# Routing steps in another order and one ring of twenty tiles for the attention output, in a fused attention and mixture-of-experts kernel

## The chip, the cores and the metric

The kernel runs on one core of a Trainium2 chip. The metric is the device time of one execution in microseconds; what is given is the median of the timed runs. One further execution was taken with the hardware profiler; all views below are of it.

## The reference

Chunked attention over 8 batches, 8 heads, 576 tokens and a head size of 64, then a mixture of experts (MoE) with noisy top-2 routing over the 8 x 576 = 4608 tokens of width 512:

```python
scores = scale * np.matmul(q_c, k_c.transpose(0, 1, 2, 4, 3))     # chunks of 64 tokens
scores = scores - np.max(scores, axis=-1, keepdims=True)
attn = np.exp(scores)
attn = attn / (np.sum(attn, axis=-1, keepdims=True) + 1e-09)
out = np.matmul(attn, v_c)
...
logits = x @ w_gate
noise_scale = np.log1p(np.exp(x @ w_noise))
noisy_logits = logits + noise_scale * noise
top2 = np.argpartition(-noisy_logits, 2, axis=1)[:, :2]
top2_l = np.take_along_axis(noisy_logits, top2, axis=1)
top2_l = top2_l - top2_l.max(-1, keepdims=True)
top2_w = np.exp(top2_l)
top2_w /= top2_w.sum(-1, keepdims=True) + 1e-09
for e in range(E):
    for k in range(2):
        mask = top2[:, k] == e
        h = np.maximum(x[mask] @ w1[e], 0.0)
        out[mask] += top2_w[mask, k, None] * (h @ w2[e])
```

There are 8 experts with a hidden size of 1024. All is float32.

## The kernel before, in words

The 4608 tokens are 36 tiles of 128 (a tile is one token per partition). The kernel has two stages, which overlap a little.

**Attention and routing.** `attend(it)` (line 726 on) is one iteration of a software pipeline, written out by hand; the engines run their instructions in the order in which this function issues them. In iteration `it` TensorE (PE) computes the scores of tile it+1 (L443), the product of the probabilities with V for tile it-2 (`pv`, L472), the transpose of the probabilities of tile it-1 (L460) and of the finished rows of tile it-3 (L488). Once in four iterations (`it % 4 == 3`) it multiplies four tiles with the gate weights (`gate_mm`, L500), and in the next iteration it turns those logits (`gate_turn`, L510). VectorE (DVE) takes the row maximum (`soft_max`, L448) and the difference (`soft_sub`, L453), up to three steps of routing, then the reciprocal (L480) and the normalisation of tile it-2 (`norm_c`, L483), which writes the tile's finished rows `xs`, then up to three more steps of routing. ScalarE (ACT) does the exponentials and the copies out of PSUM. The PSUM bank pair that `pv` writes is the one that `norm_c` of the tile before reads.

**Routing.** `route(g)` (L520) is a generator: each `yield` names the engine of the next step ("dve", "act", "pe") or asks to wait for the next iteration ("wait"). `step_route` lets it go on at fixed places of `attend`. It works on a group of four tiles (the last group has eight): softplus of the noise scale (L541 to L545), noise and logits (L547, L549), for each tile the eight largest values and their places (MAX at L555, MAX_INDEX at L559, recorded by the profile as MAX8 and as MATCH_VALUE_LOAD with FIND_INDEX8), the one-hot rows `oh` of the two chosen experts (L563 to L567), a running count by matmul (L577, L579), the two weights (L587, L590, L607), and last the row numbers `lii` (L610) to which the tokens go. When a group is through, its tiles are put on the list `pending`.

**Scattering.** `scatter` (L633) takes one entry of that list and issues on GpSimd (POOL) two short memsets (L640), a copy of one value that acts as a gate on an early result of the same iteration (L642), and an indirect DMA (L644) that writes the 128 rows of one tile, with code and weights behind each row, to the DRAM buffer `slots`; each tile is written twice, once for each of its two experts. `attend` calls it twice per iteration. Parts of `slots` are filled with zeros ahead of that, on the queue of SyncE (SP).

**The row buffers.** `rows` is a pool of five buffers, each of four tiles of 520 columns. `x_next(u)` (L435), called in the second half of every fourth iteration, takes the next buffer and sets one unused column to zero (L438). This memset is the first write to the buffer, so it stands on DVE behind the eight indirect DMAs that read the buffer's former content; the `norm_c` behind it need not wait for them any more.

**The MoE.** Tokens are gathered from `slots` by expert in blocks; x and both weight matrices are split into a high and a low part (`w_split` for the weights, L88 on ACT and L89 on DVE or POOL), and PE makes three matmuls of each product (L239). PE transposes gathered rows in `x_tile` (L222). Blocks 0 and 1 belong to the first expert and are gathered early, after groups 3 and 6 have been scattered (`load_early`, L666, gather at L171 on SP). Scatters that are left over after attention are issued between the matmuls of the first blocks. The output is accumulated by indirect DMA (L206).

Of the kernel before, what the change touches and what calls it, by code (L numbers as in the profile page):

```python
# [8 lines left out]
FT = mybir.dt.float32  # L9
# [4 lines left out]
AF = mybir.ActivationFunctionType  # L14
# [5 lines left out]
P = 128  # L20
NTOK = 4608
NT = NTOK // P
# [12 lines left out]
CODE, WA, WB, USED = DM, DM + 1, DM + 2, DM + 3  # L35
# [14 lines left out]
def kernel(ctx, tc, qT, kT, vh, wgn, noise, w1, w2, out, caps=CAPS):  # L50
    nc = tc.nc
# [15 lines left out]
    def w_load(e, which, c):  # L67
        st = stage.tile([P, 1024], FT, name="st")
        staged[e, which, c] = st
        if which == 1:  # L70
            if e == 0:
                nc.sync.dma_start(st, w1[0, c * P:(c + 1) * P, :])
            else:
                for j in range(4):
                    nc.sync.dma_start(st[32 * j:32 * j + 32], w1v[ds(place[e], 1), c, j].rearrange("o r f -> (o r) f"))
        else:
            nc.sync.dma_start(st.rearrange("p (f n) -> p f n", f=2),
                              w2[ds(place[e], 1) if e else slice(0, 1), 2 * c * P:(2 * c + 2) * P, :]
                              .rearrange("o (f p) n -> p (o f) n", f=2))
# [256 lines left out]
    pk = ExitStack()  # L336
    pv_pools = ExitStack()
    last_rows = ExitStack()
    rows = last_rows.enter_context(tc.tile_pool(name="rows", bufs=5, side="right"))
    gx = pa.enter_context(tc.tile_pool(name="gx", bufs=2, side="right"))  # L340
    work = pv_pools.enter_context(tc.tile_pool(name="work", bufs=3, side="right"))
    vs = pv_pools.enter_context(tc.tile_pool(name="vs", bufs=1, side="right"))
# [7 lines left out]
    def load_qk(j):  # L350
        if j < NT // 2:
            QB[j] = loads.tile([P, 2, 4, P], FT, name="qb", bufs=RING)
            for h in range(2):
                nc.sync.dma_start(QB[j][h::2], qT[HALF[h], 2 * j:2 * j + 2])
                nc.sync.dma_start(KB[j % RING][h::2, h], kT[HALF[h], 2 * j:2 * j + 2])

    def load_v(j):
        if j < NT // 2:
            for h in range(2):
                nc.sync.dma_start(VB[j % RING][h::2, h], vh[HALF[h], 2 * j:2 * j + 2])  # L360
# [66 lines left out]
    PR, PT, XS, XT, RC = {}, {}, {}, {}, {}  # L427
    by_head = lambda a: a.rearrange("p (g k h) -> p g h k", g=4, h=2)
    sco = [PS[:, b, :].rearrange("p (g h k) -> p g h k", g=4, h=2) for b in range(2)]

    def x_at(t):
        u, r = divmod(t, 4)
        return XS[u][:, r]

    def x_next(u):  # L435
        if 4 * u < NT:
            XS[u] = rows.tile([P, 4, 520], FT, name="xs")
            nc.vector.memset(XS[u][:, 0, USED:USED + 1], 0.0)  # L438

    def scores(t):  # L440
        for hp in range(4):
# [78 lines left out]
    def route(g):  # L520

        V = nc.vector
# [7 lines left out]
        y, u, sp = n3("gy"), n3("gu"), n3("gsp")  # L530
# [19 lines left out]
        m = gate.tile(n8, FT, name="gm")  # L550
# [15 lines left out]
        V.memset(ohb[:, G], 0.0)  # L566
        V.tensor_add(ohb[:, 0:G], oh[:, 0], oh[:, 1])  # L567
        ex, sm = nm("gex"), nm("gsm")
        yield "dve"
        V.tensor_sub(ex, m[:, :, 1], m[:, :, 0])  # L570
        if g == LAST:
            yield "wait"
            yield "wait"
# [3 lines left out]
        nc.tensor.matmul(rk, before, ohb, start=True, stop=False)  # L577
        for k in range(1, G + 1):
            nc.tensor.matmul(rk[:, k:G + 1], ones, ohb[:, 0:G + 1 - k], start=False, stop=(k == G))  # L579
        yield "act"  # L580
        nc.scalar.activation(ex, ex, AF.Exp)
        for x, s in parts:
            yield "dve"
            V.scalar_tensor_tensor(x.bitcast(I32)[:, :, CODE], mi[:, s, 0], 8192.0, tok[:, ts][:, s], op0=OP.mult, op1=OP.add)
        yield "wait"
        yield "dve"
        V.tensor_scalar(sm, ex, 1.0, 1e-9, op0=OP.add, op1=OP.add)  # L587
# [6 lines left out]
        yield "dve"  # L594
        r8 = n3("gr8")
        V.scalar_tensor_tensor(r8, rk[:, 0:G], 8.0, be(run8), op0=OP.mult, op1=OP.add)
        yield "dve"
        V.scalar_tensor_tensor(run8, rk[:, G], 8.0, run8, op0=OP.mult, op1=OP.add)
        yield "dve"
        ohr = gate.tile([P, 2, G, NE], FT, name="gohr")  # L600
# [65 lines left out]
    def load_early():  # L666
        for i, js, m in early:
            gather(i)
            early_loads.append(nc.sync.dma_start(
                meta0[i], by_slot[js * P:(js + m) * P, 0, CODE:USED].rearrange("(j p) c -> p j c", p=P)))  # L670
        early.clear()
# [54 lines left out]
    def attend(it):  # L726
        STEPS = 6
        if it % 2:
            load_qk((it - 1) // 2 + 3)
        if it % 2 == 0 and it >= 4:  # L730
            load_v((it - 4) // 2 + 3)
            if it == 32:
                load_early()
        if it in (9, 11):
            for r in range(CLEAN + 64 * (it // 2 - 4), CLEAN + 64 * (it // 2 - 3), 16):
                nc.sync.dma_start(slots[r * NE:(r + 16) * NE, 0:USED], zero)
        if it == 11:
            nc.sync.dma_start(slots[(CLEAN + P) * NE:NLIST * P * NE, CODE:USED].rearrange("(p r) c -> p r c", p=P),
                              zero[:, 0:3 * (NLIST * P - CLEAN - P) // 16].rearrange("p (r c) -> p r c", c=3))
        if it in range(4, 8):  # L740
            w_load(0, 1, it - 4)
        if it in (29, 31, 33, 35):
            w_load(0, 2, (it - 29) // 2)
        next_turn()
        if it == 0:
            scores(0)
        if it <= 1:
            p_trans(0) if it else scores(1)
        if it == 2:
            pv(0)  # L750
        if 0 < it < NT - 1:
            scores(it + 1)
        if 0 < it - 2 < NT:
            pv(it - 2)
        gated = it - 4 >= 0 and (it - 4) % 4 == 3
        if gated:
            gate_mm((it - 4) // 4)
        if 0 < it - 1 < NT:
            p_trans(it - 1)
        if 0 <= it - 3 < NT:  # L760
            x_trans(it - 3)
        if it - 5 >= 0 and (it - 5) % 4 == 3:
            gate_turn((it - 5) // 4)
            if grp_of[it - 5] != grp_of.get(it - 4):
                r = route(grp_of[it - 5])
                routing.append([r, next(r)])
        step_route("pe")
        if 0 <= it - 2 < NT:
            norm_a(it - 2)
        if 0 <= it - 1 < NT:  # L770
            p_copy(it - 1)
        if it < NT:
            mx = soft_max(it)
            soft_sub(it, mx)
            scatter(1, mx[0:1, 0, 0:1])
            soft_exp(it)
        if 0 <= it - 3 < NT:
            x_copy(it - 3)
        if gated:
            gate_copy((it - 4) // 4)  # L780
        step_route("dve", STEPS // 2)
        if 0 <= it - 2 < NT:
            norm_b(it - 2)
            scatter(1, RC[it - 2][0:1, 0, 0])
            norm_c(it - 2)
        if it - 5 >= 0 and (it - 5) % 4 == 3:
            gate_sum((it - 5) // 4)
        step_route("act")
        step_route("dve", STEPS // 2)
        if it >= 1 and (it - 1) % 4 == 0:  # L790
            x_next((it - 1) // 4)
        if it in range(33, 38):
            zero_out(3)
        if it == NT + 2:
            scatter(2, XT[(it - 3) // 4][0:1, 0, (it - 3) % 4, 0:1])
        elif it == NT + 3:
            scatter(2, LS[(it - 4) // 4][0:1, 0, 0:1])
        if it in range(7, 15):
            w_split(0, 1, *wq.pop(0), eng=nc.gpsimd)

    for it in range(NT):
# [242 lines left out]
```

## Time and profile before

| what | us |
|---|---|
| median of three timed runs (lowest, highest) | 968.83 (968.52, 969.94) |
| the profiled execution | 974.74 |
| span of its trace | 972.9 |
| busy in the span: PE / DVE / ACT / POOL | 951.2 / 457.5 / 287.3 / 236.3 |

The span runs from the first to the last record of the trace; the profiled execution's own time has some 2 us around it. PE is TensorE's matmuls, PEld its weight loads, which overlap them; DVE is VectorE, ACT ScalarE, POOL GpSimd, and SP SyncE, which only issues DMAs. In a timeline row stand the start, the duration of the merged instructions, the engine, the line of the kernel, the operation, the tile written and the tiles read, the shape, the count, and in brackets the idle time of the engine before it with what ended it. The granted clock of PE is given as a share of full speed.

### The profile page before, as it was taken

The numbers are of one execution on the slowest core, as the hardware profiler recorded it, in microseconds if no ns is written. First come the engines' busy times: TensorE is split into PE (matmuls) and PEld (weight loads), VectorE is DVE, ScalarE is ACT, GpSimd is POOL, SyncE is SP. The second block draws the span as 40 slices with busy tenths as digits, with TensorE's granted clock in tenths as the row PEclk, the third lists the DMA queues.
The fourth block names the chain that finished last, engine by engine and source line by source line (L and its number), as shares of the span: only waits on it lengthen the run. The fifth ranks groups of instructions, "written<-read, shape, count | busy, mean of one in ns | idle before, by whom it ended". The sixth has DMA issues, their size and how long they took to land. (4 is left out here: it accounts for less than half of the span.)

```text
span 972.9 us, 16180 instructions
## 1 busy us (share of the span) xinstructions
PE 951.2 (98%) x5776; PEld 846.5 (87%) x5776; DVE 457.5 (47%) x1026; ACT 287.3 (30%) x623; POOL 236.3 (24%) x426
## 2 busy tenths in 40 slices
PE   7999899999999999999999999999999999999996
PEld 6788678888897999899898989889998999899886
DVE  6798767226253542463255425443444343434311
ACT  3767553114141321241132214121312231223100
POOL 3267768430202011101111111211011011111113
PEclk9999999999999999999999999999999999999999
DMA  8999996987604632265316521652174217312213
GB/s 301 379 354 376 342 355 222 367 136 153 166 14 98 188 60 32 44 172 116 44 34 155 141 44 33 145 140 44 25 165 126 54 23 162 109 14 31 33 22 45
DMA packets 97300, 132.94 MB, mean 137 GB/s; under 512 B 23456, under 2 KB 56864, under 8 KB 97216
## 3 DMA queue, kind: packets, MB, share of 16 engines
q1 hardware_dynamic: 80160, 92.50, 31.0%
q0 software_dynamic: 16576, 38.33, 19.9%
q10 hardware_dynamic: 480, 1.05, 0.4%
q8 instruction: 46, 0.75, 0.3%
q14 instruction: 38, 0.31, 0.1%
HBM read 81.69 MB, written 50.13 MB: 135 GB/s over the span
## 5 line engine op out<-in xcount | busy, mean ns | idle before, releaser
L206 POOL DMA_INDIRECT out<-o,lid x75 | 116.7, 1557 | 647.2 <-DVE o L274 625.9
L239 PE MATMUL PS<-xh,w1h 128*128 128x384 f32 (+2 forms) x768 | 261.7, 341 | 1.9 <-issue 1.9
L239 PE MATMUL PS<-xl,w1h 128*128 128x384 f32 (+2 forms) x768 | 260.9, 340 | 0.2 <-issue 0.2
L239 PE MATMUL PS<-xh,w1l 128*128 128x384 f32 (+2 forms) x768 | 260.7, 339 | 0.0
L258 ACT ACTIVATE hh<-PS 128x384 fp32r<-128x384 f32 (+2 forms) x192 | 95.2, 496 | 463.0 <-PE PS L239 418.0
L239 PE MATMUL PS<-w2h,hh 128*128 128x512 f32 (+1 forms) x592 | 229.3, 387 | 0.0
L239 PE MATMUL PS<-w2h,hl 128*128 128x512 f32 (+1 forms) x592 | 229.1, 387 | 0.0
L239 PE MATMUL PS<-w2l,hh 128*128 128x512 f32 (+1 forms) x592 | 229.0, 387 | 0.0
L261 DVE SCALAR_TENSOR_TENSOR hl<-PS,hh 128x384 fp32r<-128x384 f32 (+2 forms) x192 | 108.6, 566 | 175.1 <-ACT hh L258 135.6
L274 DVE TENSOR_SCALAR o<-PS,lwt 128x512 f32<-128x512 f32 (+2 forms) x73 | 54.7, 749 | 224.8 <-PE PS L239 217.5
L239 PEld LDWEIGHTS PS<-xh,w1h 128*128 128x128 f32 x768 | 144.6, 188 | 8.2 <-issue 6.5
L239 PEld LDWEIGHTS PS<-xl,w1h 128*128 128x128 f32 x768 | 144.6, 188 | 2.1 <-issue 0.5
L239 PEld LDWEIGHTS PS<-xh,w1l 128*128 128x128 f32 x768 | 144.7, 188 | 1.0
L239 PEld LDWEIGHTS PS<-w2h,hl 128*128 128x128 f32 x592 | 110.8, 187 | 23.1
L239 PEld LDWEIGHTS PS<-w2l,hh 128*128 128x128 f32 x592 | 110.8, 187 | 22.2
L239 PEld LDWEIGHTS PS<-w2h,hh 128*128 128x128 f32 x592 | 110.8, 187 | 22.2
L644 POOL DMA_INDIRECT slots<-xs,lii x72 | 71.2, 989 | 26.0 <-issue 23.9
L229 ACT ACTIVATE xh<-y 128x512 fp32r<-128x512 f32 x67 | 41.2, 614 | 92.4 <-DVE y L226 90.4
L230 DVE TENSOR_TENSOR xl<-y,xh 128x512 fp32r<-128x512 f32 x67 | 44.9, 671 | 48.0 <-ACT xh L229 45.9
L443 PE MATMUL PS<-kb,qb 128*64 128x128 f32 x576 | 42.0, 291 | 9.1 <-DMA kb<-in_kT 7.1
L203 POOL MEMSET spacer<- 1x1 f32 x78 | 47.7, 612 | 0.0
L226 DVE STREAM_TRANSPOSE y<-xg 128x512 f32<-128x512 f32 x67 | 45.6, 680 | 0.0
(131 smaller groups left out, 692.8 us busy)
## 6 DMA issues: line engine op xcount, KB each, us to landing
st<-in_w SPq DMA_DIRECT2D x36, 512.0 KB
xg<-slots SPq DMA_DIRECT2D x252, 64.0 KB
st<-in_w SPq DMA_DIRECT2D x112, 128.0 KB
out<-zero SPq DMA_DIRECT2D x37, 256.0 KB
vb<-in_vh SPq DMA_DIRECT2D x36, 260.0 KB
qb<-in_qT SPq DMA_DIRECT2D x34, 256.0 KB
kb<-in_kT SPq DMA_DIRECT2D x32, 256.0 KB
xg<-slots SPq DMA_DIRECT2D x9, 256.0 KB
```

The source lines that it names most:

```text
L203: nc.gpsimd.memset(spacer, 0.0)
L206: s = nc.gpsimd.indirect_dma_start(out=to, out_offset=bass.IndirectOffsetOnAxis(ap=at[0:r], axis=0), in_=o, in_offset=None, compute_op=OP.add)
L226: nc.vector.transpose(y[:, 0:4 * r], x[:, 0:4 * r])
L229: nc.scalar.activation(oh, src, AF.Copy)
L230: nc.vector.tensor_sub(ol, src, oh.bitcast(FT))
L239: nc.tensor.matmul(p, a, b, start=first and n == 0, stop=last and n == 2)
L258: nc.scalar.activation(hh[:, 0:n], p, AF.Relu)
L261: nc.vector.scalar_tensor_tensor(hl[:, 0:n], p, 0.0, hh[:, 0:n].bitcast(FT), op0=OP.max, op1=OP.subtract)
L274: nc.vector.tensor_scalar(o[0:r], p[0:r], w, None, op0=OP.mult)
L443: nc.tensor.matmul(PS[q, t % 2, hp * P:(hp + 1) * P], QB[t // 2][:, t % 2, hp, q], KB[t // 2 % RING][:, :, t % 2, hp, q], start=True, stop ...
L644: s = nc.gpsimd.indirect_dma_start(out=slots, out_offset=bass.IndirectOffsetOnAxis(ap=lii[:, k, t0 + r:t0 + r + 1], axis=0), in_=XS[(t0 + ...
```

## The change

It has three parts, and the result is computed from the same numbers by the same operations.

1. **One ring.** The five buffers become one tile `xa` of twenty tiles of 520 columns; tile t lies at t modulo 20. `x_next` and its memset are gone. Each `norm_c` of a tile from 20 on writes its own place and itself waits for the two indirect DMAs that read the tile twenty before it.
2. **Routing steps.** The subtraction `ex` comes behind the counting matmuls instead of ahead of them, and the one ahead has no step of its own; the code (L584) is written ahead of the exponential's step; `r8` and the new count `run8` share one step. With that, routing of a group takes fewer steps: of the group whose routing begins in iteration 20 `lii` comes in the second half of iteration 24, where it came in the first half of iteration 27.
3. **First weights.** `w_split` of the first expert's first matrix is issued in iterations 6 to 13 instead of 7 to 14.

```diff
-    rows = last_rows.enter_context(tc.tile_pool(name="rows", bufs=5, side="right"))
+    rows = last_rows.enter_context(tc.tile_pool(name="rows", bufs=1, side="right"))
...
+    xa = rows.tile([P, 20, 520], FT, name="xs")
+    for u in range(NT // 4):
+        XS[u] = xa[:, 4 * (u % 5):4 * (u % 5) + 4]
+
     def x_at(t):
-        u, r = divmod(t, 4)
-        return XS[u][:, r]
-
-    def x_next(u):
-        if 4 * u < NT:
-            XS[u] = rows.tile([P, 4, 520], FT, name="xs")
-            nc.vector.memset(XS[u][:, 0, USED:USED + 1], 0.0)
+        return xa[:, t % 20]
...
         ex, sm = nm("gex"), nm("gsm")
-        yield "dve"
-        V.tensor_sub(ex, m[:, :, 1], m[:, :, 0])
         if g == LAST:
...
-        yield "act"
-        nc.scalar.activation(ex, ex, AF.Exp)
+        yield "dve"
+        V.tensor_sub(ex, m[:, :, 1], m[:, :, 0])
         for x, s in parts:
             yield "dve"
             V.scalar_tensor_tensor(x.bitcast(I32)[:, :, CODE], mi[:, s, 0], 8192.0, tok[:, ts][:, s], op0=OP.mult, op1=OP.add)
+        yield "act"
+        nc.scalar.activation(ex, ex, AF.Exp)
...
         V.scalar_tensor_tensor(r8, rk[:, 0:G], 8.0, be(run8), op0=OP.mult, op1=OP.add)
-        yield "dve"
         V.scalar_tensor_tensor(run8, rk[:, G], 8.0, run8, op0=OP.mult, op1=OP.add)
...
-        if it >= 1 and (it - 1) % 4 == 0:
-            x_next((it - 1) // 4)
...
-        if it in range(7, 15):
+        if it in range(6, 14):
             w_split(0, 1, *wq.pop(0), eng=nc.gpsimd)
```

How the order of instructions moves is shown at three places. The first is DVE from the end of iteration 21 to the normalisation of iteration 22 (tile 20), where the first used buffer is opened again. Names beginning with DMASW are the semaphores of indirect DMAs; `gm` and `gmi` are the largest logits and their places, `gsm` and `gr` the sum of the weights and the ranks. Before:

```order
L438 MEMSET xs 128x1 [waits DMASW4_49,DMASW5_49,DMASW3_49,DMASW6_49,DMASW2_49,DMASW7_49,DMASW1_49,DMASW0_49]
L448 TENSOR_REDUCE mx<-PS 128x8 [waits Pool_49]
L453 TENSOR_TENSOR pr<-PS,mx 128x4x2x64 [waits DVE_49]
L587 TENSOR_SCALAR gsm<-gex 128x4 [waits Activation_49]
L590 RECIPROCAL xs<-gsm 128x4 [waits DVE_49]
L596 SCALAR_TENSOR_TENSOR gr_1359<-PS,run_159 128x32 [waits PE_49]
L480 RECIPROCAL rc<-rc 128x8 [waits Activation_49]
L483 TENSOR_TENSOR xs<-PS,rc 128x512 [waits DVE_49,PE_49]
```

After:

```order
L553 MAX gm<-gsp 128x8 [waits DVE_49]
L553 MAX gm<-gsp 128x8
L446 TENSOR_REDUCE mx<-PS 128x8 [waits Pool_49]
L451 TENSOR_TENSOR pr<-PS,mx 128x4x2x64 [waits DVE_49]
L553 MAX gm<-gsp 128x8 x2
L557 MAX_INDEX gmi<-gm,gsp 128x8 x2
L557 MAX_INDEX gmi<-gm,gsp 128x8 [waits DVE_49] x2
L478 RECIPROCAL rc<-rc 128x8 [waits Activation_49]
L481 TENSOR_TENSOR xs<-PS,rc 128x512 [waits DMASW0_49,DMASW1_49,DVE_49,PE_49]
```

The memset with its eight semaphores is gone from ahead of the row maximum; the normalisation itself has two of them. MAX and MAX_INDEX of the group, which stood in iteration 23 before, now stand around the softmax of iteration 22; the sum of the weights and the ranks of the group before it have left this place.

The second is DVE in iteration 24 from behind the subtraction to the end of the iteration (`goh` and `gohb` are one-hot arrays, `lg` the logits of the next group). Before:

```order
L563 TENSOR_TENSOR goh<-e_row,gmi 128x32
L566 MEMSET gohb 128x4
L567 TENSOR_TENSOR gohb<-goh 128x32
L570 TENSOR_TENSOR gex<-gm 128x4
L480 RECIPROCAL rc<-rc 128x8
L483 TENSOR_TENSOR xs<-PS,rc 128x512
L517 TENSOR_REDUCE lg<-PS 128x64
```

After:

```order
L585 TENSOR_SCALAR gsm<-gex 128x4
L588 RECIPROCAL xs<-gsm 128x4
L594 SCALAR_TENSOR_TENSOR gr_1510<-PS,run_159 128x32
L595 SCALAR_TENSOR_TENSOR run_159<-PS,run_159 128x8
L478 RECIPROCAL rc<-rc 128x8
L481 TENSOR_TENSOR xs<-PS,rc 128x512
L515 TENSOR_REDUCE lg<-PS 128x64
L598 TENSOR_TENSOR gohr<-goh,gr_1510 128x64
L601 COPY lim_87<-run_159 128x1
L604 TENSOR_TENSOR xs<-gex,xs 128x4
L607 TENSOR_REDUCE lii<-gohr 128x2x4
```

The one-hot rows have left the iteration, and the whole end of the routing, from the sum of the weights to the row numbers `lii`, has come into it.

The third is POOL from the last splits of the first weights to the second scatter. Before:

```order
L89 TENSOR_TENSOR w1l_821<-st,w1h_820 128x512
L640 MEMSET spacer 1x1 x2
L642 COPY spacer<-rc 1x1
L644 DMA slots<-xs,lii 44032x576
L89 TENSOR_TENSOR w1l_821<-st,w1h_820 128x512
L640 MEMSET spacer 1x1 x2
L642 COPY spacer<-mx 1x1
L644 DMA slots<-xs,lii 44032x576
```

After:

```order
L89 TENSOR_TENSOR w1l_774<-st,w1h_773 128x512
L637 MEMSET spacer 1x1 x2
L639 COPY spacer<-mx 1x1
L641 DMA slots<-xs,lii 44032x576
L637 MEMSET spacer 1x1 x2
L639 COPY spacer<-rc 1x1
L641 DMA slots<-xs,lii 44032x576
L89 TENSOR_TENSOR w1l_774<-st,w1h_773 128x512
```

Before, one scatter stands ahead of the last split; after, two do, and the first is gated by a row maximum (`mx`) of iteration 13 instead of by an `rc` of iteration 14.

## The prediction

> **What bounds the kernel now.** First the page, for the engine that fills the span.
>
> ```profile
> span 972.9 us, 16180 instructions
> PE 951.2 (98%) x5776; PEld 846.5 (87%) x5776; DVE 457.5 (47%) x1026; ACT 287.3 (30%) x623; POOL 236.3 (24%) x426
> ```
>
> TensorE (PE) is busy for 951.2 us of 972.9, so a change can only win what lies in its 21.7 us of gaps, and what its slow clock costs. Next a table of busy time by windows, cut where the stages and the clock change (columns: window, length, busy time of PE, PEld, DVE, ACT, POOL, granted clock, DMA share, GB/s).
>
> ```profile
> 57.00:109.50 52.50, 52.41 (x692) 43.97 (x692) 45.41 (x184) 34.21 (x87) 37.01 (x106) 1.00 1.01 371
> 109.50:113.45 3.95, 1.44 (x22) 1.10 (x22) 3.04 (x13) 1.44 (x3) 2.81 (x9) 1.00 1.04 412
> 113.45:116.86 3.41, 3.41 (x24) 1.41 (x21) 2.92 (x17) 0.27 (x1) 2.28 (x9) 0.50 0.94 332
> 174.00:178.30 4.30, 2.17 (x11) 1.48 (x10) 0.69 (x1) 0.60 (x1) 2.50 (x6) 1.00 1.03 391
> 178.30:181.72 3.42, 3.42 (x13) 3.42 (x12) 1.31 (x2) 0.49 (x1) 0.28 (x2) 0.50 1.04 390
> 200.00:900.00 700.00, 700.00 (x3545) 630.09 (x3544) 303.37 (x503) 181.70 (x380) 104.61 (x132) 1.00 0.43 91
> ```
>
> From 200 to 900 PE has no gap: nothing the change does there counts. It loses time at two places, near 110 (attention) and 174 (second block of the MoE), and each time 3.41 us at half clock follow, worth 3.41 / 2 = 1.7 us. In attention DVE is busy 45.41 of 52.5 us, so it has little spare. What DVE waits for at 110:
>
> ```profile
> 107.24 0.19 DVE L549 TENSOR_TENSOR gsp<-gsp,lg 128x32 f32<-128x32 f32 x1
> 110.13 0.06 DVE L438 MEMSET xs<- 128x1 f32 x1 [2.69 <-DMA slots<-xs,lii]
> 110.86 0.69 DVE L453 TENSOR_TENSOR pr<-PS,mx 128x512 f32<-128x512 f32 x1
> ```
>
> and what PE does then:
>
> ```profile
> 109.02 0.60 PE L488 MATMUL PS<-ident,xs 128*128 128x128 f32 x4
> 111.60 1.09 PE L443 MATMUL PS<-kb,qb 128*64 128x128 f32 x16 [1.98 <-DVE pr L453]
> 113.23 1.76 PE L472 MATMUL PS<-vb,pts 128*64 128x130 f32 x15 [0.54 <-DVE xs L483]
> ```
>
> The memset that opens a row buffer of four tiles waits 2.69 us for row writes of the tiles that lay there; the softmax of the iteration stands behind it on DVE, and PE stands idle 1.98 + 0.54 = 2.52 us. All waits of that memset together:
>
> ```profile
>   DMA slots<-xs,lii: 3.1, 3
> ```
>
> so the other two are worth 0.4 us.
>
> How much attention loses in all is read from the start of the scores (L443) at every fourth iteration, from iteration 8 on:
>
> ```profile
> 32.25 1.09 PE L443 MATMUL PS<-kb,qb 128*64 128x128 f32 x16
> 46.21 1.09 PE L443 MATMUL PS<-kb,qb 128*64 128x128 f32 x16
> 60.15 1.09 PE L443 MATMUL PS<-kb,qb 128*64 128x128 f32 x16
> 73.61 1.09 PE L443 MATMUL PS<-kb,qb 128*64 128x128 f32 x16
> 86.94 1.09 PE L443 MATMUL PS<-kb,qb 128*64 128x128 f32 x16
> 100.21 1.09 PE L443 MATMUL PS<-kb,qb 128*64 128x128 f32 x16
> 117.88 1.09 PE L443 MATMUL PS<-kb,qb 128*64 128x128 f32 x16
> ```
>
> The periods are 13.96, 13.94, 13.46, 13.33, 13.27 and 17.67 us. The shortest, 13.27, is a period without loss; above it lie 0.69, 0.67, 0.19, 0.06, 0 and 4.40. The last is the stall with its half clock (2.52 + 1.7 = 4.2).
>
> **Part 1, the ring.** Nine memsets of 0.06 us go. The wait moves to the normalisation (L483) of tile t, which then waits for the two row writes of tile t-20 alone. Are these landed? POOL's writes form a chain from the first to the end of attention:
>
> ```profile
> 57.42 1.17 POOL L644 DMA_INDIRECT slots<-xs,lii  x1 [0.95 <-DMA qb<-in_qT]
> 103.08 0.98 POOL L644 DMA_INDIRECT slots<-xs,lii  x1 [0.42 <-issue]
> 108.78 0.98 POOL L644 DMA_INDIRECT slots<-xs,lii  x1 [0.45 <-issue]
> 161.16 0.99 POOL L644 DMA_INDIRECT slots<-xs,lii  x1 [0.16 <-issue]
> ```
>
> 103.08 is number 23 (from 0) and 108.78 number 26: 5.7 / 3 = 1.90 us each. The waiting memset needed number 23, the last of its buffer, which let it go at 110.1, seven microseconds after its issue. Tile 28, the first to use the buffer again, needs only numbers 16 and 17 (tile 8), which by the chain start at about 103.08 - 7 x 1.90 = 89.8 and 91.7 and so have landed by 99; its normalisation comes in iteration 30, after 104 (iteration 28 starts at 100.21). Each later tile gains one iteration (some 3.3 us) and needs two writes more (3.8 us), so the margin shrinks by 0.5 us a tile, from over 5 us to about 2 us at tile 35. I count the stall as gone: what is then late next is DVE itself (part 2). The added semaphores of 16 normalisations on DVE: an opening memset had eight, so fewer are waited on at a time; I take 0 to 0.1 us each on DVE (the two short waits of the memset were 0.2 each with eight), and 0.1 us in all on PE's path, since most of it falls into iterations where DVE has slack. Should such a wait last, the logits' sum, routing steps and the next softmax stand behind it on DVE, and PE waits for all of these and for the PSUM banks that the normalisation frees.
>
> Nothing here starts a write earlier at the front: the first has its idle time ended by a DMA, and it comes after the zero fills of `slots`. Scatters are emitted five places ahead of before but run in the same chain, so writes up to the end of attention keep their times.
>
> **Part 2, the order of routing.** The same instructions run, drawn together. Call the iterations of a period 0 to 3, 0 being that of the logits' turn (`it` a multiple of 4). In the first turn of routing (group 0) the old program already stood as all groups now stand: two MAX behind the normalisation of iteration 1, two MAX and four MAX_INDEX between subtraction and reciprocal of iteration 2. DVE there:
>
> ```profile
> 40.01 0.69 DVE L448 TENSOR_REDUCE mx<-PS 128x8 f32<-128x512 f32 x1
> 41.34 0.23 DVE L555 MAX8 gm<-gsp 128x8 f32<-128x8 f32 x2
> 41.95 0.16 DVE L559 FIND_INDEX8 gmi<-gm,gsp 128x8 uint32<-128x8 f32 x1
> 42.03 0.18 DVE L480 RECIPROCAL rc<-rc 128x8 f32<-128x8 f32 x1
> 42.31 0.69 DVE L483 TENSOR_TENSOR xs<-PS,rc 128x512 f32<-128x512 f32 x1
> ```
>
> and PE's:
>
> ```profile
> 38.55 1.09 PE L443 MATMUL PS<-kb,qb 128*64 128x128 f32 x16
> 41.65 1.09 PE L443 MATMUL PS<-kb,qb 128*64 128x128 f32 x16
> 43.15 1.11 PE L472 MATMUL PS<-vb,pts 128*64 128x130 f32 x16 [0.41 <-DVE xs L483]
> ```
>
> From 41.34 to 42.03 DVE does nothing but MAX and MAX_INDEX, so the normalisation that follows starts at 42.31; it frees the PSUM banks that the product with V (L472) of iteration 3 writes, which starts 0.84 us later, 0.41 us late. That period lost 0.69 us (above), and it lacks the work that a steady one has at its start (the weights and ranks of the group before), so I take 0.7 as the lower and 0.9 as the upper end, and 0.8 for each of the six later periods: 6 x 0.8 = 4.8 us. What before lost in the same six: 0.67 + 0.19 + 0.06 + 0 + 4.40, and 1.01 in the last one, whose row is
>
> ```profile
> 128.31 1.11 PE L472 MATMUL PS<-vb,pts 128*64 128x130 f32 x16 [1.01 <-DVE xs L483]
> ```
>
> together 6.3 us. The bounds of a period's loss for the range, wider than mine: 0 (DVE catches up in iteration 3, which now has two routing rows) and 1.5 (rival B).
>
> The rule for the clock bears on this. In this trace 2.52 us of idle PE within 3.6 us (109.6 to 113.2) dropped the clock, and 1.91 at 174.7 did; the 1.01 at 127.3 did not. The Trainium skill, "TensorE: Matmul & The Clock Gate", section "HAM oscillation — how this bites in real kernels", puts the limit at idle gaps above about 3.4 us; by it the half clock after a stall of 2.5 us would have another cause and stay, and the sum would lose its 1.7 us and come to +0.3 us. The trace disagrees with the limit; the length it shows, 3.41 us, is the window that the page's Part 1 gives.
>
> **Part 3, the split of the first weights one iteration earlier.** Same instructions on ACT and POOL. The last one on POOL,
>
> ```profile
> 54.49 1.27 POOL L89 TENSOR_TENSOR w1l<-st,w1h 128x512 fp32r<-128x512 f32 x1 [1.21 <-ACT w1h L88]
> ```
>
> now stands behind two scatters, so it runs after 57.42 + 1.90 = 59.3; its weights are used only when attention's products are through, past the 128.31 above. Zero.
>
> **Behind attention.** PE's gain can be eaten at the first tile of MoE block 1, whose rows are gathered once write number 55 is out (161.16 above):
>
> ```profile
> 163.93 1.31 SPq L171 DMA_DIRECT2D xg<-slots  x3
> 167.01 0.49 PE L222 MATMUL PS<-ident,xg 128*128 128x128 f32 x3
> ```
>
> Landing comes just ahead of 167.01, so this point is tight. Five scatters more are emitted within attention, so number 55 is gated by an earlier turn of the MoE; numbers 26 to 55 took 161.16 - 108.78 = 52.4 us, 1.8 each, and I estimate the gather about one write earlier, 1.7 us, at most. That caps PE's gain at 1.7 unless more goes later. The stall at 174.7
>
> ```profile
> 176.61 0.41 PE L239 MATMUL PS<-xh,w1h 128*128 128x384 f32 x1 [1.91 <-issue]
> ```
>
> is put down to nothing the profile shows; I leave it as it is.
>
> **The sum:** +4.8 - 6.3 + 0.1 = -1.4 us in the profiled execution: span 972.9 to 971.5, run 974.74 to 973.3. The median of the timed runs, 968.83, is 5.9 us below that run; I take -1.4 from it as well: 967.4. Under 0.2% (1.94 us, about what a measurement of this kernel can tell from no change).
>
> **Rivals.**
>
> A, faster. DVE makes good the bunching in the slack of iteration 3, so nearly all of the 6.3 is won; the gather caps it at 1.7; but then the second stall, a coincidence of a busy DMA (share 1.03 at 174 to 178) with a PE that arrives at that moment, also goes, with its half clock: -1.7 - 1.9 - 1.7 = -5.3, 963.5; half of that stall gone gives 965.4. For it: the spare time of iteration 3, and that no wait shows why PE stood still at 174.7. Against: group 0 had the same spare time and lost 0.69. Chance 0.29.
>
> B, slower. The bunched MAX and MAX_INDEX hold V's product back by more than in group 0, because weights, rank sum and `lii` now precede them on DVE in the same period. It decides once the delay is over 6.3 / 6 = 1.05 us a period. At 1.5 us each (0.69 plus about four more routing rows of 0.2) it is 9.0 - 6.3 = +2.7, 971.5; should two gaps in one period add up to what dropped the clock here (between 1.01 and 1.91 us), 1.7 us a period come on top, to about 980 for six. The Trainium skill, same page, section "A second HAM failure mode: psum-queue depth-cycling", tells of a clock that swings between its two states from frequent short gaps; no gap of 1.01 us or less does so here. B also covers timed runs in which the stall at 110 is smaller than in the profiled one. Against B: DVE has idle time in a steady period, as in iteration 0 of the one from 86.94:
>
> ```profile
> 89.56 0.20 DVE L480 RECIPROCAL rc<-rc 128x8 f32<-128x8 f32 x1 [0.25 <-ACT rc L477]
> ```
>
> That iteration keeps four routing rows, and iteration 3 gives up the MAX rows and `lii`, and keeps two. Chance 0.23.
>
> C, the change does not do what it says: the writes of a tile are still out when its normalisation comes (the margin of 2 us at tile 35 would have to be wrong), so one wait takes the other's place, at up to 2.5 us, and time stays within 1 us of before, 968.8. The margin of 5 us at tile 28 speaks against it. Chance 0.04.
>
> **The numbers.** My forecast has 0.44 (0.40 of it within 0.2%, 0.04 beyond, where a period's loss is under 0.7). Faster: 0.04 + 0.29 = 0.33; same: 0.40 + 0.04 = 0.44; slower: 0.23. Range: A's two ends lie at 963.5 and 965.4, B's first at 971.5; 963.8 to 971.5 leaves out the far end of each, about 0.1 on either side. The forecast's own range, by 0.7 to 0.9 a period, is 966.8 to 968.0.
>
> **What would show it.** Right: no wait of DVE for row writes; periods of about 14.1 us from 46 to 126, each with a short idle of PE ahead of L472 in iterations 2 and 3; no half clock near 113; attention ending about 1.4 us earlier; the gather of block 1 at about 162. Wrong: periods of 13.3 (A) or above 14.4 (B), a granted clock of 0.5 inside attention, or a normalisation idle ahead of which a row write stands.

## The result and the profile after

The changed kernel is slower: 976.08 us (median of four runs, 974.01 to 977.01) against 969.38 us for the kernel before in the same series (968.52 to 970.80), a ratio of 1.0063 with a 95% interval of 1.0045 to 1.0081. The forecast was 967.4 us and its range ended at 971.5; both the range and the side were wrong. Measured again in another series (e10 below) the ratio was 1.0054 (1.0041 to 1.0067).

The page after, its first two lines:

```profile
span 972.2 us, 16177 instructions
PE 947.7 (97%) x5776; PEld 843.4 (87%) x5776; DVE 459.9 (47%) x1017; ACT 287.9 (30%) x623; POOL 236.1 (24%) x431
```

The profiled execution is the shortest of the four (974.01 us), while that of before (974.74) was longer than all four timed runs of before. So the two spans, 972.2 and 972.9, say the opposite of the timed runs, and the difference has to be looked for by stages. First the three largest of PE's waits up to 180 us (columns: total, times, longest; the loads of k at the start, 7.5 us, are left out):

```profile
PE PS L470 <- DVE xs L481: 2.9, 5, 1.4
PE PS L222 <- DMA xg<-slots: 1.9, 1, 1.9
PE PS L508 <- ACT ls L502: 1.9, 1, 1.9
```

and two rows of the same list before:

```profile
PE PS L472 <- DVE xs L483: 2.6, 4, 1.0
PE PS L239 <- issue: 2.1, 2, 1.9
```

The wait for the softmax behind the memset is gone, as forecast. New are one of 1.9 us for gathered tokens and one of 1.9 us for the logits' copy; the waits for normalisations are five with 2.9 us in all, where they were four with 2.6. Gone, which was not forecast, is also the stall at 174.7 (L239) with its half clock: after, PE is busy for all of the 45.00 us from 155 to 200. The starts of the scores, as in the prediction, for comparison from iteration 8 on (L441 now):

```profile
31.75 1.09 PE L441 MATMUL PS<-kb,qb 128*64 128x128 f32 x16
45.49 1.09 PE L441 MATMUL PS<-kb,qb 128*64 128x128 f32 x16
60.65 1.09 PE L441 MATMUL PS<-kb,qb 128*64 128x128 f32 x16
74.75 1.09 PE L441 MATMUL PS<-kb,qb 128*64 128x128 f32 x16
88.64 1.09 PE L441 MATMUL PS<-kb,qb 128*64 128x128 f32 x16
102.58 1.09 PE L441 MATMUL PS<-kb,qb 128*64 128x128 f32 x16
116.75 1.09 PE L441 MATMUL PS<-kb,qb 128*64 128x128 f32 x16
```

The periods are 13.74, 15.16, 14.10, 13.89, 13.94 and 14.17 us: about 14.1, as forecast, except the second. Attention is 117.88 - 116.75 = 1.1 us ahead of the profile before. The loss comes where attention passes into the MoE. A write of POOL and the gather on SP's queue there:

```profile
126.74 0.98 POOL L641 DMA_INDIRECT slots<-xs,lii  x1 [0.45 <-issue]
```

```profile
129.50 1.32 SPq L171 DMA_DIRECT2D xg<-slots  x3
```

and the same gather before:

```profile
122.97 1.32 SPq L171 DMA_DIRECT2D xg<-slots  x3
```

126.74 is write number 37, and in the built program the first gather's semaphore stands at number 37; before it stood at 32, and the gather left at 122.97. Block 0 needs the writes up to 31 only, but the gather is issued in iteration 32 and waits for every write issued ahead of it, now five more. ACT a little later, before and then after:

```profile
141.22 0.63 ACT L88 ACTIVATE w2h<-st 128x512 fp32r<-128x512 f32 x1
```

```profile
144.76 0.63 ACT L88 ACTIVATE w2h<-st 128x512 fp32r<-128x512 f32 x1 [2.98 <-POOL spacer L639]
```

the last copy of an `rc` on POOL, before and then after:

```profile
138.83 0.18 POOL L642 COPY spacer<-rc 1x1 f32<-1x1 f32 x1 [0.86 <-DVE rc L480]
```

```profile
144.55 0.18 POOL L639 COPY spacer<-rc 1x1 f32<-1x1 f32 x1
```

and PE after:

```profile
132.54 0.66 PE L222 MATMUL PS<-ident,xg 128*128 128x128 f32 x4 [1.86 <-DMA xg<-slots]
145.93 0.66 PE L508 MATMUL PS<-ident,ls 128*128 128x128 f32 x4 [1.85 <-ACT ls L502]
```

ACT's first split of w2 waits for a copy on POOL, the one that ends at 144.73; before, that copy was over at 139.01 and the split started without a wait. The weights' pool takes the memory that the attention's work tiles leave, among them `mx` and `rc`, which POOL's copies read as gates of the writes. In the built program this split waits for POOL's count 160, before for 145: fifteen instructions, five writes of three. The copy of the logits stands behind the split on ACT, and PE waits for it. Neither wait was in the prediction.

The first profile before is that of a long run. Held against the second one (e1 below, 971.01 us), matmul by matmul, PE of the changed kernel is 1.2 us late at 122 us, 5.7 late at 153 and 3.0 late from 177 to the end: the passage takes 4.5, and the stall at 174, which e1 has too, gives 2.7 back. These two profiled runs differ by 3.0 us, the medians by 5.7 (e10) and 6.7; what makes up the rest is not shown, and why the stall is gone is not either.

### The profile page after: what moved, and what is told of

The parts are those of the page before. It is cut to its first block, busy times and chain, and to the rows that moved or that the text cites. A ratio compares the mean times of both kernels' runs of the same rounds, so it can differ in the third digit from the quotient of the medians.

```text
span 972.2 us, 16177 instructions
## 1 busy us (share of the span) xinstructions
PE 947.7 (97%) x5776; PEld 843.4 (87%) x5776; DVE 459.9 (47%) x1017; ACT 287.9 (30%) x623; POOL 236.1 (24%) x431
## 3 DMA queue, kind: packets, MB, share of 16 engines
q10 hardware_dynamic: 480, 1.05, 0.3%
## 5 line engine op out<-in xcount | busy, mean ns | idle before, releaser
L239 PE MATMUL PS<-xh,w1h 128*128 128x384 f32 (+2 forms) x768 | 261.0, 340 | 0.0
L239 PE MATMUL PS<-xh,w1l 128*128 128x384 f32 (+2 forms) x768 | 260.1, 339 | 0.0
L239 PE MATMUL PS<-xl,w1h 128*128 128x384 f32 (+2 forms) x768 | 260.1, 339 | 0.0
L239 PE MATMUL PS<-w2h,hh 128*128 128x512 f32 (+1 forms) x592 | 229.3, 387 | 0.0
L239 PE MATMUL PS<-w2h,hl 128*128 128x512 f32 (+1 forms) x592 | 229.1, 387 | 0.0
L239 PE MATMUL PS<-w2l,hh 128*128 128x512 f32 (+1 forms) x592 | 229.0, 387 | 0.0
L239 PEld LDWEIGHTS PS<-xh,w1h 128*128 128x128 f32 x768 | 144.1, 188 | 5.9 <-issue 4.2
L239 PEld LDWEIGHTS PS<-xl,w1h 128*128 128x128 f32 x768 | 144.1, 188 | 1.7
L239 PEld LDWEIGHTS PS<-xh,w1l 128*128 128x128 f32 x768 | 144.1, 188 | 1.0
L239 PEld LDWEIGHTS PS<-w2h,hl 128*128 128x128 f32 x592 | 110.8, 187 | 23.1
L239 PEld LDWEIGHTS PS<-w2l,hh 128*128 128x128 f32 x592 | 110.8, 187 | 22.3
L239 PEld LDWEIGHTS PS<-w2h,hh 128*128 128x128 f32 x592 | 110.8, 187 | 22.1
L441 PE MATMUL PS<-kb,qb 128*64 128x128 f32 x576 | 40.9, 287 | 7.6 <-DMA kb<-in_kT 7.5
L89 DVE TENSOR_TENSOR w2l<-st,w2h 128x512 fp32r<-128x512 f32 x64 | 44.3, 692 | 3.1 <-DMA st<-in_w 3.1
```

Source lines behind the costliest of these rows:

```text
L89: (eng or nc.vector).tensor_sub(lo[:, s], st[:, s], hi[:, s].bitcast(FT))
L239: nc.tensor.matmul(p, a, b, start=first and n == 0, stop=last and n == 2)
L441: nc.tensor.matmul(PS[q, t % 2, hp * P:(hp + 1) * P], QB[t // 2][:, t % 2, hp, q], KB[t // 2 % RING][:, :, t % 2, hp, q], start=True, stop ...
```

## Experiments

Each ratio is to the kernel before in the same series, fifteen runs in all. Each series ran on a chip of its own. The kernel before had medians of 972.4 us in that of e1 to e4 and 973.0 in that of e5 to e8, with a wide spread, and of 969.0 and 969.2 in those of e9 to e12 and of e13 to e15; so differences of a few us between a run of the first two and one of the last two are not used.

| kernel | median us | ratio (95% interval) |
|---|---|---|
| e1 before again | 972.81 | 1.0013 (0.9997 to 1.0029) |
| e2 ring alone | 971.74 | 0.9997 (0.9982 to 1.0012) |
| e3 order alone | 977.44 | 1.0059 (1.0040 to 1.0077) |
| e4 gather in iteration 30 | 976.21 | 1.0048 (1.0030 to 1.0066) |
| e5 writes held back | 977.77 | 1.0051 (1.0031 to 1.0072) |
| e6 gates apart, gather in 30 | 972.94 | 1.0009 (0.9990 to 1.0027) |
| e7 before, late gather | 973.31 | 0.9997 (0.9977 to 1.0016) |
| e8 ring, gates apart | 971.15 | 0.9984 (0.9970 to 0.9999) |
| e9 gates apart alone | 976.58 | 1.0066 (1.0048 to 1.0085) |
| e10 changed kernel again | 974.74 | 1.0054 (1.0041 to 1.0067) |
| e11 e8, gather at once | 970.20 | 1.0007 (0.9998 to 1.0016) |
| e12 e8, one spacer | 965.07 | 0.9958 (0.9945 to 0.9972) |
| e13 e12, new order | 970.92 | 1.0018 (1.0009 to 1.0027) |
| e14 e13, spread | 966.53 | 0.9970 (0.9959 to 0.9980) |
| e15 e13, early splits | 971.24 | 1.0020 (1.0011 to 1.0028) |

**e1, the kernel before once more.** No edit.

> The kernel before, unchanged, for a second profile. The profiled run of before was 974.74 us, 5.9 above its median. If the 2.5 us stall at the buffer's memset and the 1.9 us stall at 174.7 with their half clocks belong to every run, this profile shows both again. If they are accidents of that one run, the profiled run comes out near 969 and at least one of the two is missing; then the reordered kernel had nothing of it to win.

The profiled run took 971.01 us, span 969.2, and the stall that the ring was to win is small there. DVE, then PE:

```profile
109.25 0.06 DVE L438 MEMSET xs<- 128x1 f32 x1 [1.03 <-DMA slots<-xs,lii]
```

```profile
110.73 1.09 PE L443 MATMUL PS<-kb,qb 128*64 128x128 f32 x16 [0.37 <-DVE pr L453]
112.35 1.11 PE L472 MATMUL PS<-vb,pts 128*64 128x130 f32 x16 [0.53 <-DVE xs L483]
174.46 0.41 PE L239 MATMUL PS<-xh,w1h 128*128 128x384 f32 x1 [1.95 <-issue]
```

The memset waits 1.03 us instead of 2.69, PE 0.9 instead of 2.52, no window between the kernel's start and its end runs at half clock, and the period is 115.41 - 100.95 = 14.46 us, 1.2 above the shortest instead of 4.4. The second stall, of 1.95 us, is there again, but no half clock follows it. Of the first profile's 4.4 us, 3.2 did not come again.

**e2 and e3, the change in halves.** e2 has the ring of the diff alone, e3 the diff of `route` alone.

> The ring of twenty tiles alone; routing order and weight splits as before. Theory: block 0's gather waits for write number 32 as before and DVE's work is spread as before, so the time is 965 if the memset's stall is in every run of before (2.5 us and 1.7 us of half clock won), 969 if it is an accident. Rival, that the semaphores of the normalisations cost time: above 971.

> The routing order alone; five buffers with their memsets and the weight splits as before. Theory: it carries the whole loss, by the gather of block 0 that now waits for write 37 instead of 32 (about 4 us at the passage to the MoE) and by 0.6 to 0.9 us a period on DVE: 975 to 977. Rival, that the ring is what costs: 969 to 970.

The ring alone changes nothing that can be measured; the order alone carries the whole loss. e2's 971.74 us lies above the 971 that its expectation gave to the rival that the new semaphores cost, but the kernel before itself took 972.4 in that series; the ratio of 0.9997 leaves that rival no room.

**e4, e9 and e6, the two waits at the passage.** e4 moves the gather, e9 the gates' tiles, e6 has both edits:

```diff
-            if it == 32:
+            if it == 30:
                 load_early()
...
-        mx = work.tile([P, 4, 2], FT, name="mx", bufs=6)
+        mx = gx.tile([P, 4, 2], FT, name="mx", bufs=6)
...
-        RC[t] = work.tile([P, 2, 4, 1], FT, name="rc", bufs=6)
+        RC[t] = gx.tile([P, 2, 4, 1], FT, name="rc", bufs=6)
```

> The changed kernel with block 0's gather issued in iteration 30 instead of 32, so that it waits for write 33 instead of 37. Theory of the gather: it is issued near 123.5 instead of 129.5, the waits of 1.86, 1.85 and 0.79 us behind it go, and the time falls from 976 to 972. Rival, that the bunched routing steps are the whole loss: 976, with the gather early and PE late all the same.

> The changed kernel with mx and rc in the pool that lives on, and the gather left in iteration 32: the gates' half of e6 alone. Theory, that the late gather and ACT's wait for POOL's copies hide each other: PE's wait at the gathered tile (1.9 us) stays, its wait for the logits (1.9 us) goes, and it lies 2.5 to 4 above before, between the changed kernel (6) and e6 (1). Rival, that the gates' wait is the whole loss: as e6, within 1.5 above before.

> The changed kernel with the gather in iteration 30, and the small tiles mx and rc that gate the writes allocated in a pool that lives on, so that the first split of w2 has not to wait for POOL's copies of them. Theory: ACT's split starts near 142 instead of 145, the wait of PE for the logits behind it (2.64 us in e4) goes, and it lies 2 to 3 us above before. Rival, that ACT waits there for the load of w2 and not for POOL: the wait stays and it lies 4.5 to 5 above before, as e4.

Either edit alone wins little or nothing (1.0048 and 1.0066), less than each theory expected; both together bring the kernel level with before (1.0009), more than expected. That level is against a slow and scattered before (969.2 to 978.5 us); e13, in a quiet series, says 1.0018 with both waits gone. What PE waited for from 120 to 160 us in e4, the gather left at 122.28:

```profile
PE PS L508 <- ACT ls L502: 2.6, 1, 2.6
PE PS L470 <- DVE xs L481: 1.4, 1, 1.4
PE PS L470 <- DMA vb<-in_vh: 0.9, 1, 0.9
```

and in e9:

```profile
PE PS L222 <- DMA xg<-slots: 3.0, 1, 3.0
PE PS L470 <- DVE xs L481: 1.4, 1, 1.4
PE PS L573 <- DVE gohb L565: 0.8, 1, 0.8
```

With the gather early the wait behind POOL's copies is 2.6 us instead of 1.9: PE that does not wait at the first comes earlier to the second. So the first wait hides a part of the second, and e4 alone would have led to dropping the gather from the causes. e9's longer first wait, 3.0 us, is another matter, since it lies ahead of the second in time: its gather left at 131.00 instead of 129.50, for a reason that is not shown. In both profiles a window at half clock follows the wait that is left.

**e5, the writes held to their old places; e7, the late gather in the kernel before.** e5 lets no write leave ahead of its place before (a test of the iteration in `scatter`); e7 moves `load_early` to iteration 33.

> The changed kernel, but no write of rows is issued ahead of its place in the program before (group 0 from the second half of iteration 14, group g from that of iteration 4g + 15). So block 0's gather waits for write 32 again, and five gate copies fewer are issued on POOL before the first split of w2 may reuse their memory. Theory of two causes (passage to the MoE about 4 us, bunched routing on DVE about 2.5): the waits of 1.86, 1.85 and 0.79 us go, and it lies 2 to 3 us above before instead of 6. Rival, bunching alone: 6 above. Rival, the passage alone: level with before.

> The kernel before with block 0's gather issued in iteration 33 instead of 32, behind write 34 instead of 32, so near 129 instead of 123. Theory, that the late gather costs of itself: PE waits 1 to 2 us at its transposes and the weights' loads behind it on SP come 6 us later; 1.5 to 3 above before. Rival, that this wait only hides the one for the gate copies: level with before (within 1).

Both missed the theory. In e5 the waits for the gather and for the logits go, but the first write leaves at 60.02 us instead of 54.45, since PE reaches its place later, the chain of writes ends later with it, and another wait stands at 166.6 (1.79 us for a split of w2 on DVE behind the end of the routing, with a half clock after it); so it says nothing on the share of the passage. In e7 PE does wait for the gather:

```profile
130.53 0.66 PE L222 MATMUL PS<-ident,xg 128*128 128x128 f32 x4 [1.48 <-DMA xg<-slots]
```

and the time is level with before all the same. Its gather left at 127.49, that of e9 at 131.00, where PE waited 3.0 us. So in the kernel before a gather that is late by 4.5 us is borne. Whether one that is late by 8 would be, e9 cannot tell, since it has the new order too; what each wait would cost alone in the changed kernel is not settled.

**e10, the changed kernel again.**

> The changed kernel unchanged, beside the others on one chip. Theory: 5 to 6.5 above before again; PE's waits of 1.4, 1.9, 1.9 and 0.8 us between 127 and 155 stand in its profile as in the first one, and whether a half-clock window of 3.4 us follows one of the two long ones is chance, as it was absent in the first profile. Rival, that the first measurement was an accident of its chip: within 2 of before.

The loss is there again. Its profile has the wait for the gather (1.87 us) and, unlike the first, a window at half clock behind it (rows below); the wait for the logits is not among those over 0.35 us this time.

**e8, e11 and e12, the ring without the new order.** e8 is e2 with e9's edit. e11 issues the gather in `scatter` behind write 31. e12 is e8 with

```diff
-            for _ in range(2 if attending[0] else 1):
+            for _ in range(1):
```

> The ring with the old routing order, and mx and rc in the pool that lives on: a candidate for the fastest. Theory: ACT's first split of w2 no longer waits for POOL (0.78 us in e2), PE's 0.58 us wait for ranks behind it goes too: 0.5 to 1.5 us below before. Rival, that these waits are covered: level with e2 and before.

> The kernel of e8 (ring, old routing order, gates apart) with block 0's gather issued right behind write 31, the last that it needs, instead of at iteration 32. Theory: the gather comes 2 us earlier, PE's 0.54 us wait for it goes, 0 to 0.7 us below e8, so 1.5 to 2.5 below before. Rival: the loads behind it on SP come late and hold PE at the last V tiles: above e8.

> The kernel of e8 with one spacer memset ahead of a write during attention instead of two. Theory: the writes run closer, 1.8 us apart or less instead of 1.90, until DVE's and ACT's gates hold them back; the gathers of blocks 0 and 1 come 1 to 4 us earlier, PE's waits for them (0.54 and 1.59 us in e8) go: 2 to 4 below before. Rival, that the writes then take the DMA from the loads of k, q and v, whose waits grow: level with before or above.

e8 is faster than before by 0.0016 at the edge of its interval; e11 is no better, its loads of V come late (PE waits 3.79 us at 130.63). e12 is the fastest kernel here, 965.07 us: write 31 leaves at 111.3 instead of 118.0 (e8), no wait for a gather is left, and PE stands still nowhere for over 0.35 us from 60 to 120.

**e13, e14 and e15, the order by itself.** e13 puts the new order (with its splits, and the gather in iteration 30) on e12, where neither wait at the passage is left. e14 gives each MAX and each MAX_INDEX a step of its own, and has the gather in iteration 32 again:

```diff
-            if r % 2 == 0:
-                yield "dve"
+            yield "dve"
             V.max(m[:, r], sp[:, r])
...
-            if r % 2 == 0:
-                yield "dve"
+            yield "dve"
             V.max_index(mi[:, r], m[:, r], sp[:, r])
```

e15 issues two splits in each of iterations 6 to 9 instead of one in 6 to 13.

> e12 (ring, gates apart, one spacer) with the new routing order and splits, and the gather in iteration 30: of the change only what it does on DVE is left against e12. Theory, bunching costs of itself: periods of 13.9 us with PE waiting 0.4 us for a normalisation in each, and 2.5 to 4 us above e12 (so 1.5 below to level with before). Rival, that only the two waits at the passage to the MoE cost: level with e12, 4 below before.

> e13 with a step of its own for every MAX and MAX_INDEX (two more half steps each), gather in iteration 32, which then waits for write 33. Theory of the bunching: no more than two MAX or three MAX_INDEX stand between a subtraction and a reciprocal, the periods fall to 13.3 to 13.5 and the time to within 1 of e12. Rival, that the number of routing rows in a period is what costs and not where they stand: periods and time as e13.

> e13 with the first weights split in iterations 6 to 9, two in each, instead of one in each of 6 to 13. In the profiles of the reordered kernels two-input rows of DVE took 1.29 and 1.96 us instead of 0.19 and 0.28 while POOL's subtraction of a split ran, in the period from iteration 12. Theory, that the two engines hold each other up there: that period falls from 15.1 to 13.9, 1 us below e13, less what the splits cost before iteration 9. Rival, that the period's first writes hold DVE up: 15 as before.

The order alone costs 970.92 - 965.07 = 5.9 us, in two series in which before had 969.0 and 969.2; 2.5 to 4 were expected. PE in e13, in e12 and in e14 over one period:

```profile
72.48 1.11 PE L470 MATMUL PS<-vb,pts 128*64 128x130 f32 x16 [0.38 <-DVE xs L481]
75.64 1.09 PE L441 MATMUL PS<-kb,qb 128*64 128x128 f32 x16
89.52 1.09 PE L441 MATMUL PS<-kb,qb 128*64 128x128 f32 x16
```

```profile
73.04 1.09 PE L441 MATMUL PS<-kb,qb 128*64 128x128 f32 x16
86.31 1.09 PE L441 MATMUL PS<-kb,qb 128*64 128x128 f32 x16
```

```profile
72.69 1.09 PE L441 MATMUL PS<-kb,qb 128*64 128x128 f32 x16
86.04 1.09 PE L441 MATMUL PS<-kb,qb 128*64 128x128 f32 x16
```

13.88, 13.27 and 13.35 us. The rows of routing are as many in all three; it is where they stand that costs. Over the six periods e13 loses 84.30 - 80.65 = 3.6 us to e12, the rest behind them (among it waits of 1.41 and 0.74 us for DVE at 128 and 152). e14 wins 4.4 of the 5.9 back, in the same series as e13; its gather is later than e13's and its gain therefore not the gather's.

e15 moves a cost and does not remove it. Its starts:

```profile
32.56 1.09 PE L441 MATMUL PS<-kb,qb 128*64 128x128 f32 x16
47.85 1.09 PE L441 MATMUL PS<-kb,qb 128*64 128x128 f32 x16
61.73 1.09 PE L441 MATMUL PS<-kb,qb 128*64 128x128 f32 x16
```

The period from iteration 12 falls from 14.98 (e13) to 13.88, that from iteration 8 rises from 13.75 to 15.29.

## Why the prediction was wrong, point by point

**The ring (part 1).** Its mechanism held: no wait for a row write is left on DVE, so no margin ran out. Its size failed, and this step turned the side of the forecast: the 4.40 us of one period were taken for what every run loses. e1 shows 1.2, and e2 that the time does not change. The text had the sign of it: the profiled run was 5.9 us above the median of the timed runs, and this was carried along as an offset ("I take -1.4 from it as well") where it said that the run was not a usual one. Two windows of half clock stood in it, 3.4 us together.

**The bunching (part 2).** Right in place and nearly in size: 4.8 us forecast for six periods, 0.69 us each read from group 0; measured 5.9 us in e13 against e12, and in the changed kernel's profile 85.00 - 6 x 13.27 = 5.4 us, of which 0.5 are group 0's, and 1.4 behind them, 6.3 in all. The period from iteration 12 was the one missed: it lost 1.9 us, of which 1.1 went when e15 took the splits away from it (14.98 to 13.88), since POOL's subtraction of a split holds up small rows of DVE (below).

**"Nothing here starts a write earlier ... writes up to the end of attention keep their times."** The times of the writes were right within 3 us, and the conclusion from them, that the passage to the MoE costs nothing, was wrong. Five writes more are issued ahead of two fixed places of the program, the gather in iteration 32 and the end of the work pool, and both wait for all that stand ahead of them. The tight point that I named, block 1's gather, came 2.5 us earlier (161.40) and cost nothing; block 0's, where I looked at no semaphore, came 6.5 us later. With both waits removed the ratio falls from 1.0063 to 1.0009 (e6), or 1.0018 with the writes closer together as well (e13). The sum had no term for the passage; held against e1's profile it takes 4.5 us, some 0.5 of it a normalisation's.

**Part 3** cost nothing that can be told: e3, without it and without the ring, loses as much as the whole change. No run tests it alone.

**The clock.** The sum had 1.7 us for a half clock that goes. In the profiles here such a window comes and goes with the run; it is a price of every long gap of PE times a chance, and the change added two long gaps at the passage and took one away at 174.

**The rivals.** B had the side, though only in part by its mechanism: four of the six periods lost 0.6 to 0.9 us each, less than its decision point of 1.05. That point was worked out from the 6.3 us of the one long run; with e1's 3.7 us it lies at 0.6, under the forecast's own 0.8. With e1's term the same sum would have given 4.8 - 3.7 + 0.1 = +1.2. Of A one half came: the stall at 174.7 went with its half clock, which the sum had left as it was; that DVE makes good the bunching did not come. C did not occur.

**The signs.** Nearly all that was named as a sign of being right was seen: no wait of DVE for row writes, periods of about 14.1 us but for one, a short idle of PE ahead of the product with V in each (one, not two), no half clock inside attention, attention 1.1 us earlier, the gather of block 1 at 161.40. All of them look at attention or at block 1; none looked at the passage, or at whether the run that they were held against was a usual one.

## What to carry to other kernels

Before a stall of one profile is put into a sum, hold the profiled run against the timed ones: if it is longer by about the size of the stall, the stall may be an accident of that run, and a second profile tells. An instruction that is moved ahead of a fixed place in the program is waited for there, here by a load and by the reuse of memory; so for everything that is issued earlier, list what waits for "all before", on every queue. Steps drawn together on an engine that is busy for 86% of a stage delay that stage even if none is added, and of two waits in a row the first can hide the second, so that they must be removed together before their price shows.

## What the runs showed of the hardware

**The clock goes by windows, not by gaps.** In the profile before, the two half-clock windows start at 113.45 and 178.30, 64.85 us apart, which is 19 x 3.413. Taken as a grid of 3.413 us, each follows a window in which PE was idle for over half. Shown are pairs of windows on the grid, of before, of e10 and of e8:

```profile
174.88:178.30 3.42, 1.47 (x7) 1.24 (x8) 0.69 (x1) 0.60 (x1) 1.84 (x4) 1.00 1.03 390
178.30:181.72 3.42, 3.42 (x13) 3.42 (x12) 1.31 (x2) 0.49 (x1) 0.28 (x2) 0.50 1.04 390
```

```profile
130.10:133.53 3.43, 1.56 (x24) 1.29 (x23) 0.00 (x0) 2.60 (x6) 2.52 (x8) 1.00 1.02 339
133.53:136.94 3.41, 3.41 (x23) 3.07 (x18) 1.99 (x7) 1.52 (x4) 2.40 (x6) 0.50 1.01 322
```

```profile
161.66:165.07 3.41, 1.82 (x11) 1.26 (x10) 0.00 (x0) 0.00 (x0) 2.82 (x6) 1.00 0.87 264
165.07:168.50 3.43, 3.43 (x19) 2.83 (x18) 1.69 (x3) 1.20 (x2) 2.77 (x7) 1.00 1.03 378
```

Idle for 1.95 and 1.87 us of a window, the clock halves in the next; idle for 1.59, it does not. Between 100 and 950 us, the profiles of all seventeen runs have eight windows at full clock in which PE is idle for 1.79 us or more, each followed by a half clock, and none of those with 1.67 or less is. A window that is itself at half clock needs less: e11 has one with 1.4 us idle, and the clock stays at half for another. One window with 1.87 near 20 us, in e5, is not followed by a half clock, which stays open. e1's gap of 1.95 us is cut by the grid, counted from 965.3 us, where its clock falls at the end of the kernel:

```profile
170.00:173.41 3.41, 2.50 (x14) 1.79 (x11) 0.00 (x0) 0.00 (x0) 2.96 (x5) 1.00 1.04 397
173.41:176.83 3.42, 2.15 (x11) 1.93 (x12) 0.92 (x2) 0.60 (x1) 1.13 (x4) 1.00 1.04 390
176.83:180.24 3.41, 3.41 (x22) 3.41 (x21) 1.36 (x3) 0.98 (x2) 1.58 (x5) 1.00 1.03 386
```

0.91 and 1.27 us idle, and the clock stays. So a gap of the same length costs 1.7 us more (half of the 3.41) in some runs and not in others. The Trainium skill, "TensorE: Matmul & The Clock Gate", section "What's actually happening", says that the window is free-running and 3413 ns long, which the traces bear out; the rule of the section "HAM oscillation — how this bites in real kernels", that gaps above about 3.4 us count, they do not.

**A subtraction on POOL holds up small rows of DVE.** In the changed kernel, DVE and then POOL:

```profile
51.24 1.29 DVE L541 TENSOR_TENSOR gsp<-gsp,gu 128x32 f32<-128x32 f32 x1
52.57 0.19 DVE L543 SCALAR_TENSOR_TENSOR gsp<-lg,gsp 128x32 f32<-128x32 f32 x1
57.08 1.96 DVE L561 TENSOR_TENSOR goh<-e_row,gmi 128x32 f32<-128x32 f32 x2
```

```profile
51.20 1.28 POOL L89 TENSOR_TENSOR w1l<-st,w1h 128x512 fp32r<-128x512 f32 x1 [2.04 <-ACT w1h L88]
57.60 1.28 POOL L89 TENSOR_TENSOR w1l<-st,w1h 128x512 fp32r<-128x512 f32 x1
```

The kernel before has one such row:

```profile
54.82 0.99 DVE L541 SCALAR_TENSOR_TENSOR gu<-gu,gy 128x32 f32<-128x32 f32 x1
```

A row that takes 0.19 us in other periods takes 1.29, or 0.99 before, and a pair of 0.28 takes 1.96; each ends within 0.2 us of the end of POOL's subtraction. POOL's row takes 1.27 to 1.29 us in every run, so it is DVE that is held up. The pair starts 0.52 us ahead of the subtraction, while POOL issues a write; what held it that early is not shown. The Trainium skill, "SBUF — State Buffer", section "Terms", tells of a port pair that the two engines lock against each other for a whole instruction; the first of these rows fits it, and e15, where the cost moved with the splits (a row at 38.62 takes 1.30 us there), does too.
